# Fixing the order and metering the pace of a scan's VectorE work inside a fused SSM and feed-forward kernel

## The chip, the cores and the metric

One core of one Trainium2 chip. The metric is the device time of one execution in microseconds (us). "The span" is the time from the first to the last instruction in the profile; it lies 1 to 2 us under the measured time. Lower is better.

The engines are called PE (TensorE, the matmuls), DVE (VectorE), ACT (ScalarE), POOL (GpSimd) and SP (SyncE, which here only issues transfers).

## The reference, cut to what matters

```python
xn = layernorm(x)                                    # 2048 x 1024
# A: state-space model (SSM), 1024 complex states
Bu = einsum("bld,pd->blp", xn, B_bar)                # complex
for t in range(2048):                                # the scan
    h = Lam_bar * h + Bu[:, t]
y  = 2.0 * einsum("blp,dp->bld", hseq, C).real + xn * Dskip
# B: feed-forward network (FFN), 1024 -> 3584 -> 1024
f  = (silu(xn @ w_gate) * (xn @ w_up)) @ w_down
out = x + y + f
```

The kernel turns the complex scan into two real ones: each block of 128 states and 512 time steps (a *unit*, 32 in all) is rotated by a table of cosines and sines, scanned with a real decay, and rotated back. The tables are built by doubling, on DVE.

## The kernel before

Four parts matter: the start (load x, layernorm, transpose x through PE), the B matmuls as one block, the scan on DVE, and the FFN. The source writes the whole scan ahead of the FFN; a scheduler that models the engines decides in what order each engine really gets its instructions. The two products that the FFN needs from DVE carry a high priority.

```python
with tc.tile_pool(name="ph0_x", bufs=2, side="right") as ph0x, ...:
    for j4 in range(0, NTT, JTB):                     # four chunks of x, 1 MB each
        xt = ph0x.tile([P128, JTB, D], BF16, name="xt", tag="xt")
        nc.sync.dma_start(xt[:], x_view[:, j4 : j4 + JTB, :])
        xts.append(xt)
    nc.sync.dma_start_transpose(BT[:, 0, :, :], A_B_re)   # all of B at once
    nc.sync.dma_start_transpose(BT[:, 1, :, :], A_B_im)
    # ... per chunk: sums (ACT), squares (DVE), normalise (DVE), 32 transposes (PE),
    #     eight evictions of the transposed x into xnT (ACT)

for blk in range(NPB):                                # 8 blocks of states
    for tb in range(NTB):                             # 4 blocks of time
        ups = bups.tile([P128, 2, TBLK], FP32, name="ups", tag="ups")
        # ... 16 matmuls of 128x128x512; eviction by ACT; store to u_dram

for g in range(NPG):                                  # two blocks of states at a time
    # ... build the tables (DVE, six operations per doubling)
    for bb in range(NBG):
        for tb in range(NTB):
            # ... one unit on DVE: 6 products, 2 scans, 4 small carries, 6 products;
            #     load of u and store of h by POOL

for tq in range(NTQ):                                 # FFN, four quarters of the rows
    for fpair in range(NFP):                          # 14 pairs, 28 gate/up blocks
        # ... loads of wg and wu (pool f_w, bufs=2), 16 matmuls, 3 evictions (ACT)
        with tc.high_priority(offset=BOOST):
            nc.vector.tensor_tensor(out=gsb[:], in0=gsb[:], in1=sig[:], op=ALU.mult)
            nc.vector.tensor_tensor(out=prodT[...], in0=gsb[:], in1=usbf[:], op=ALU.mult)
    for q in range(NQ):                               # down projection, 448 matmuls
        # ...
# output stage: 4 reads of h (2 MB each), 512 matmuls with C, sum, store
```

## Time and profile before

| | before |
|---|---|
| time, median of the first 4 runs | 919.9 us (918.99 to 921.04) |
| span | 918.5 us |
| PE busy | 827.7 us (90%) |
| DVE busy | 477.8 us (52%) |
| PE work at full speed (worked out in the prediction) | 810.4 us |
| lost: start / middle / tail | 46.8 / 57.1 / 4.2 us |

PE is the engine that should never pause. DVE's 52% is an average of two stages: nearly full until about 360 us, nearly empty after. The prediction shows the slices and the pauses; it has 57.4 and 3.9 for the last two losses, but the last matmul of the lines that it shows ends at 914.35 us, 4.2 before the end of the span. Two more views help. First, the shares of the chain that ended last, in the kernel before:

```profile
PE 65%; DVE 26%; issue 3%; DMA 3%; SPq 1%; ACT 0%; POOL 0%; POOLq 0%; DVEq 0%
```

A quarter of the path to the end runs through DVE, though PE is the busier engine. Second, what PE waited for in the kernel before (total us, times, longest us):

```profile
PE gps L378 <- ACT gsb L395: 24.1, 11, 15.3
PE gps L378 <- DMA wg<-in_B_w_gate_dram: 15.7, 2, 15.2
PE dps L412 <- DVE prodT L400: 7.6, 3, 3.4
```

The first line names ACT, but ACT itself was waiting for a tile that DVE's products had not yet released.

### The profile page before, as it was taken

The page shows a single profiled execution, that of the slowest core. Times are in us where ns is not written, and L with a number is a line of the kernel's source. Part 1 is how long each engine was busy: PE and PEld are TensorE (multiplying, and loading weights), DVE is VectorE, ACT ScalarE, POOL GpSimd, SP SyncE. Part 2 cuts the span into 40 slices and gives each one's busy share as a digit, 9 for nine tenths or more (in the row PEclk, how much of TensorE's full clock was granted, in tenths as well). Part 3 has the DMA queues.
Part 4 walks back from the last instruction along what each step waited for, and adds up shares of the span by engine and source line. Part 5 has one row for each costly group of instructions (what it writes and reads, how often), then busy time and mean ns, then how long its engine had stood idle before and what let it go on. Part 6 is the DMA issues. An engine that isn't in the chain of part 4 may idle for free.

```text
span 918.5 us, 12444 instructions
## 1 busy us (share of the span) xinstructions
PE 827.7 (90%) x4736; PEld 461.8 (50%) x4736; DVE 477.8 (52%) x1291; ACT 286.2 (31%) x508; POOL 38.7 (4%) x74
## 2 busy tenths in 40 slices
PE   0669999759887897599999999999999999999998
PEld 0334444324333784244488544468744458844443
DVE  5799999999999997022200122210022220076563
ACT  5662332234433113144421354431244541100000
POOL 1002101100110100000000000000000000000000
PEclk9979999969999899699999999999999999999999
DMA  9997433865664483955546754546665523356631
GB/s 232 232 193 237 141 112 138 247 198 162 201 185 143 139 238 129 314 143 145 159 137 168 197 158 138 161 124 182 178 173 147 149 80 101 103 172 209 207 109 42
DMA packets 239788, 152.08 MB, mean 166 GB/s; under 512 B 38960, under 2 KB 219184, under 8 KB 239728
## 3 DMA queue, kind: packets, MB, share of 16 engines
q1 hardware_dynamic: 220608, 121.65, 48.3%
q0 software_dynamic: 5296, 17.05, 5.7%
q10 hardware_dynamic: 13824, 12.59, 4.1%
q8 instruction: 37, 0.61, 0.3%
q14 instruction: 23, 0.19, 0.1%
HBM read 117.71 MB, written 25.17 MB: 156 GB/s over the span
## 4 chain that ended last, share of the span: by engine, by line
PE 65%; DVE 26%; issue 3%; DMA 3%; SPq 1%; ACT 0%; POOL 0%; POOLq 0%; DVEq 0%
PE dps L412 21%; PE gps L378 15%; PE upsf L386 15%; PE yacc L455 12%; DVE ww L322 4%; DVE ln_scr L194 1%; DMA wg<-in_B_w_gate_dram 1%; DMA xt<-in_A_x_dram 1%; DVE prodT L400 1%; DVE gsb L399 1%; SPq L369 1%; DVE vv L319 1%; DMA lre_b<-in_A_Lambda_re_dram 1%; DVE ectab L278 1%; DVE hst L345 1%
## 5 line engine op out<-in xcount | busy, mean ns | idle before, releaser
L378 PE MATMUL gps<-xnT,wg 128*128 128x512 bf16 x896 | 215.0, 383 | 40.0 <-ACT gsb L395 24.1
L386 PE MATMUL upsf<-xnT,wu 128*128 128x512 bf16 x896 | 213.0, 381 | 0.0
L412 PE MATMUL dps<-wdq,prodT 128*128 128x256 bf16 x1792 | 198.4, 274 | 7.6 <-DVE prodT L400 7.6
L412 PEld LDWEIGHTS <-prodT 128*128 128x128 bf16 x1792 | 175.9, 98 | 30.2 <-DVE prodT L400 8.4
L399 DVE TENSOR_TENSOR gsb<-gsb,sig 128x512 bf16<-128x512 bf16 x112 | 47.5, 424 | 254.7 <-ACT gsb L395 254.7
L378 PEld LDWEIGHTS <-wg 128*128 128x128 bf16 x896 | 88.1, 98 | 149.8 <-issue 27.4
L386 PEld LDWEIGHTS <-wu 128*128 128x128 bf16 x896 | 88.1, 98 | 107.4 <-issue 2.9
L393 ACT ACTIVATE sig<-gps 128x512 bf16<-128x512 f32 x112 | 66.9, 597 | 168.3 <-PE gps L378 109.0
L234 PE MATMUL ups<-xnT,BT 128*128 128x512 bf16 x512 | 116.7, 383 | 0.0
L455 PE MATMUL yacc<-CT,hread 128*128 128x512 bf16 x512 | 110.7, 379 | 0.0
L397 ACT ACTIVATE usbf<-upsf 128x512 bf16<-128x512 f32 x112 | 66.8, 596 | 58.7 <-PE upsf L386 58.7
L400 DVE TENSOR_TENSOR prodT<-gsb,usbf 128x512 bf16<-128x512 bf16 x112 | 47.5, 424 | 71.0 <-ACT usbf L397 70.6
L322 DVE TENSOR_TENSOR_SCAN ww<-rdec,carry,vv 128x512 bf16<-128x512 f32 x64 | 81.9, 1283 | 0.0
L455 PEld LDWEIGHTS <-hread 128*128 128x128 bf16 x512 | 50.1, 98 | 60.2
L419 ACT ACTIVATE dstg<-dps 128x256 bf16<-128x256 f32 x64 | 24.5, 383 | 175.7 <-PE dps L412 155.4
L234 PEld LDWEIGHTS <-BT 128*128 128x128 bf16 x512 | 50.4, 99 | 56.9
L395 ACT ACTIVATE gsb<-gps 128x512 bf16<-128x512 f32 x112 | 66.5, 594 | 21.6 <-DVE prodT L400 21.6
L242 ACT ACTIVATE ust<-ups 128x1024 bf16<-128x1024 f32 x32 | 32.7, 1022 | 70.6 <-PE ups L234 65.6
L218 PE MATMUL tp<-ident,xt 128*128 128x128 bf16 x128 | 15.7, 255 | 39.0 <-DVE xt L210 37.3
L463 DVE TENSOR_TENSOR oacc<-yacc,pre 128x512 bf16<-128x512 f32 x32 | 22.1, 691 | 43.8 <-PE yacc L455 43.8
L218 PEld LDWEIGHTS <-xt 128*128 128x128 bf16 x128 | 11.3, 113 | 47.5 <-DVE xt L210 39.9
L435 DVE TENSOR_SCALAR c<-dskb,rstd 128x1024 bf16<-128x1024 bf16 x16 | 7.7, 480 | 47.8 <-PE dps L412 47.8
(104 smaller groups left out, 435.1 us busy)
## 6 DMA issues: line engine op xcount, KB each, us to landing
wg<-in_B_w_gate_dram SPq DMA_DIRECT2D x56, 512.0 KB, 3.7
wu<-in_B_w_up_dram SPq DMA_DIRECT2D x56, 512.0 KB, 4.9
wdq<-in_B_w_down_dram SPq DMA_DIRECT2D x16, 1792.0 KB, 8.7
u_dram<-ust ACTq DMA_DIRECT2D x32, 256.0 KB, 2.1
usb<-u_dram POOLq DMA_DIRECT2D x32, 256.0 KB, 3.3
h_dram<-hst POOLq DMA_DIRECT2D x32, 256.0 KB, 2.9
hread<-h_dram SPq DMA_DIRECT2D x4, 2048.0 KB, 9.9
xt<-in_A_x_dram SPq DMA_DIRECT2D x4, 1024.0 KB, 8.7
```

What stands on the lines that cost most here:

```text
L234: nc.tensor.matmul(ups[:, ri, :], lhsT=BT[:, ri, dk, blk * P128 : (blk + 1) * P128], rhs=xnT[:, dk, t0 : t0 + TBLK], start=(dk == 0), stop ...
L242: nc.scalar.activation(ust[:], ups[:], ACT.Copy)
L322: nc.vector.tensor_tensor_scan(ww[:, ri, :], rbc, vv[:, ri, :], carry[:, tb, blk, ri : ri + 1], ALU.mult, ALU.add,)
L378: nc.tensor.matmul(gps[:], lhsT=wg[:, dk, fl * P128 : (fl + 1) * P128], rhs=xnT[:, dk, tcol : tcol + TBLK], start=(dk == 0), stop=(dk == N ...
L386: nc.tensor.matmul(ups2[:], lhsT=wu[:, dk, fl * P128 : (fl + 1) * P128], rhs=xnT[:, dk, tcol : tcol + TBLK], start=(dk == 0), stop=(dk == ...
L393: nc.scalar.activation(sig[:], gps[:], ACT.Sigmoid)
L395: nc.scalar.activation(gsb[:], gps[:], ACT.Copy)
L397: nc.scalar.activation(usbf[:], ups2[:], ACT.Copy)
L399: nc.vector.tensor_tensor(out=gsb[:], in0=gsb[:], in1=sig[:], op=ALU.mult)
L400: nc.vector.tensor_tensor(out=prodT[:, ft_idx, tbq * TBLK : (tbq + 1) * TBLK], in0=gsb[:], in1=usbf[:], op=ALU.mult,)
L412: nc.tensor.matmul(dps[:], lhsT=prodT[:, ft_idx, jl * P128 : (jl + 1) * P128], rhs=wdq[:, ft_idx, :], start=(ft_idx == 0), stop=(ft_idx == ...
L455: nc.tensor.matmul(acc[:], lhsT=hread[:, blk, ri, tt * P128 : (tt + 1) * P128], rhs=CT[:, ri, blk, dh * 512 : (dh + 1) * 512], start=(i == 0),
```

## The change

The intent: let PE always have work and DVE never be late with a product. The order of instructions on DVE and on the SP queue is no longer left to the scheduler. The program writes it: after each block of PE work it emits a bounded amount of scan work, by a meter that counts PE time. The parts:

```diff
+    ph0x = tc.alloc_tile_pool(name="ph0_x", bufs=4, side="right")       # was bufs=2
+    # B is transposed per block of 128 states (bt_pool, bufs=2), not all at once
+    def emit_bu(n):
+        for _ in range(n):
+            ...                                  # one B unit: 16 matmuls, eviction, store
+        def build_table(blk): ...                # one block at a time, four operations per doubling
+        def do_unit(kcur): ...                   # 6 products, 2 scans, carries
+        def end_unit(kcur): ...                  # 6 products, store of h
+        ssm_steps = []
+        for blk in range(NPB):
+            ssm_steps.append((6.0, (lambda b=blk: build_table(b))))
+            for tb in range(NTB):
+                kk = units.index((blk, tb))
+                ssm_steps.append((5.2, (lambda k2=kk: do_unit(k2))))
+                ssm_steps.append((2.5, (lambda k2=kk: end_unit(k2))))
...
+            def advance(self, pe_us):
+                self.budget += pe_us * 0.5
+                while self.idx < len(ssm_steps) and self.budget >= ssm_steps[self.idx][0]:
+                    cost, fn = ssm_steps[self.idx]
+                    ...
+                    self.budget -= cost
+                    self.idx += 1
+                    fn()
...
+        dve_order = tc.manual_schedule(engines={mybir.EngineType.DVE, mybir.EngineType.SP})
+        dve_order.__enter__()
+        emit_bu(3)
+        ssm_driver.advance(30.0)
...
-                tc.tile_pool(name="f_w", bufs=2) as fw, \
+                tc.tile_pool(name="f_w", bufs=3) as fw, \
...
+                    if bu_state["k"] < NU:
+                        emit_bu(BU_PER_PAIR)     # three B units in each of the first pairs
...
-                            with tc.high_priority(offset=BOOST):
-                                nc.vector.tensor_tensor(out=gsb[:], ...)
+                            nc.vector.tensor_tensor(out=gsb[:], ...)
...
+                            ssm_driver.advance(GU_US + ...)      # after each gate/up block
...
+                        if tq < 2:               # C transposes, one pair per part of a down projection
+                            nc.sync.dma_start_transpose(CT[:, 0, po, :], ...)
...
+                            ssm_driver.advance(DP_US)            # after each down group
```

## The prediction

> **What bounds the kernel now.** I read the slices first, for where TensorE (PE) is not full; the stretches for how much; the PE timeline for each pause; then the chain and the groups for what the work costs when nothing is in its way.
>
> The slices of the page, 23 us each:
>
> ```profile
> PE   0669999759887897599999999999999999999998
> DVE  5799999999999997022200122210022220076563
> PEclk9979999969999899699999999999999999999999
> ```
>
> PE is at 9 from slice 18 on, and pauses only in slices 0 to 17. In just these slices VectorE (DVE) is at 9, and after slice 16 it has almost nothing to do. So the kernel is bound by PE, and what it loses, it loses while DVE works through the whole scan part of the state-space model (SSM).
>
> The stretches: bounds, length, busy us and instructions of PE, PEld, DVE, ACT, POOL, then granted clock, DMA share, GB/s:
>
> ```profile
> 0.00:69.00 69.00, 29.99 (x199) 16.59 (x200) 54.12 (x214) 43.64 (x79) 5.11 (x12) 0.90 1.03 219
> 69.00:161.00 92.00, 92.00 (x428) 41.72 (x427) 90.83 (x254) 26.60 (x26) 12.61 (x24) 1.00 0.46 156
> 161.00:391.00 230.00, 182.34 (x1025) 101.48 (x1023) 201.55 (x558) 67.43 (x123) 20.95 (x39) 0.91 0.67 196
> 391.00:804.00 413.00, 413.00 (x2579) 252.23 (x2578) 66.12 (x157) 148.28 (x280) 0.00 (x0) 1.00 0.53 147
> 804.00:914.00 110.00, 110.00 (x512) 49.81 (x509) 64.46 (x111) 0.25 (x1) 0.00 (x0) 1.00 0.46 152
> ```
>
> PE is idle 39.0 us in the first stretch and 47.7 in the third. In the fourth, 413 us, DVE has 66 us of work.
>
> What full speed is, from the chain (start, length, what) and one row of the PE timeline:
>
> ```profile
> 512.63 1.73 PE gps L378 x8
> 463.72 48.91 PE dps L412 x448
> 803.83 110.52 PE yacc L455 x512
> 63.53 100.96 PE L234 MATMUL ups<-xnT,BT 128*128 128x512 bf16 x467
> ```
>
> A gate or up group of 8 matmuls is 1.73 us (two such, one gate/up block, 3.45), a down projection 48.9, the output projection 110.5, a matmul of B times u 0.216. The work at full speed: 112 blocks x 3.454 = 386.8; 4 x 48.91 = 195.6; 110.5; 512 x 0.216 = 110.5; 128 transposes at 0.055 (four in 0.22 us in the timeline) = 7.0. Sum 810.4 us. The span is 918.5, so 108.1 are lost. Before 63.5 us PE did 45 of the B matmuls and the transposes, 16.7 us of work: 46.8 lost at the start. After the last matmul 3.9. The rest, 57.4, is lost between 164 and 391: 47.7 idle, the remainder at a lower clock and on groups cut up.
>
> The pauses themselves, in the PE timeline (in brackets the idle time before, and what ended it):
>
> ```profile
> 23.57 1.47 PE L218 MATMUL tp<-ident,xt 128*128 128x128 bf16 x6 [23.57 <-DVE xt L210]
> 52.91 1.76 PE L218 MATMUL tp<-ident,xt 128*128 128x128 bf16 x8 [13.45 <-DVE xt L210]
> 193.61 3.57 PE L378 MATMUL gps<-xnT,wg 128*128 128x512 bf16 x8 [15.31 <-ACT gsb L395]
> 249.21 1.89 PE L378 MATMUL gps<-xnT,wg 128*128 128x512 bf16 x8 [1.16 <-ACT gsb L395]
> 300.96 47.57 PE L412 MATMUL dps<-wdq,prodT 128*128 128x256 bf16 x421 [3.29 <-DVE prodT L400]
> 377.57 3.59 PE L378 MATMUL gps<-xnT,wg 128*128 128x512 bf16 x8 [15.23 <-DMA wg<-in_B_w_gate_dram]
> ```
>
> 23.57 is the first load and layernorm; 13.45 the third chunk of x, whose load could not start until one of two buffers was free (issued at 31.7 us, behind 24 us of B-transpose issue on the same queue). 15.31 and the 1.16 kind are one thing: ScalarE (ACT) waits for its tile because the two FFN products on DVE stand behind scan work. 15.23 is the queue: several 1.8 MB down weights and a 2 MB read of h were issued together, and the issue of the gate weights behind them took 11.5 us.
>
> **What the Trainium skill says.** "TensorE: Matmul & The Clock Gate", Part 1, says PE runs at half clock after an idle window of about 3.4 us until it has been busy as long. The trace agrees: after the 15.31 pause the first eight matmuls took 3.57 us, later ones 1.89, and the three long pauses are the slices at 6 and 7 of the clock row. Each long pause thus costs some 2 to 3 us more. "Perfetto Trace Analysis", Per-engine timelines, says ACT and DVE are strict FIFO; the trace agrees, as products ready for 15 us run after scan work already queued. "VectorE: DVE Perf Modes", the perf-mode tier table, caps fp32 tensor-tensor at one element per cycle and lets fp32 tensor-scalar have two; the trace has 690 ns for 512 fp32 elements of the first and 482 of the second. That bears on the new tables.
>
> **The change, part by part.** (1) All four x loads have buffers and go first; B is transposed per block of 128 rows, two small transposes each, rather than 24 us of issue at once. This takes away the 13.45 pause. What is left is the rate of ACT and DVE: ACT has 16 sums x 1.05 (start to start) + 32 evictions x 0.54 + 4 table loads x 1.28 = 39 us from 6.5 us on, five B evictions at 1.02, and I allow 3 to 4 of waits, so it ends near 54. DVE has 16 x 1.15 + 16 x 0.46 + 10 of small operations = 36 from 10 us. PE starts at 23 as before; until 54 it can do the transposes (7) and up to six B units of 3.45 (20.7): 27.7. The rest is in order behind them, and the FFN's PSUM banks overlap those of the transposes (four B banks, two for transposes, four for the FFN are more than eight). Loss at the start: 54 - 27.7 = 26, plus 2 for the cold clock and 2 for poor order: 30 in place of 46.8. Gain 17.
>
> (2) The B units are no longer a block of 92 us that only PE works in; three go in each of the first ten FFN pairs. PE's work does not change by that, gain 0 in itself. It gives DVE 92 us more FFN time to hide behind.
>
> (3) The scan is metered: after each block of PE time t it may emit t/2 of DVE work, and DVE and the SP queue run in the order written. A scan unit is 12 products at 0.335 (start to start), 2 scans at 1.20, 0.5 of carries = 7.0 us; the meter says 5.2 + 2.5. A table now has per doubling two tensor-scalars and two fused operations; about 0.55 us for each of six small levels, 0.7, 1.0 and 1.4 for the large, 2.8 for casts and the last four = near 9 us an estimate; the meter says 6. Total 32 x 7.0 + 8 x 9 = 296 us, as the meter has it (294), so it takes 590 us of PE time and ends in the fourth quarter, well ahead of the output stage. In a plain block of 3.45 us DVE has 0.75 of products and 1.73 of scan: 72%. The longest thing in front of a product is a table, 9 us. PE has two PSUM tiles and ACT two SBUF tiles of lead, so the product of block i must be done before PE wants block i+4: about 3 blocks less 2.5 us of ACT and DVE, 7.9 us after its inputs. So nearly nothing reaches PE. At the four turns to the down projection the last product is wanted 2.95 us after the block; a unit of 5 us just ahead of it costs 1 to 2, a table up to 6: 6 in all. The 15.31 and the many small pauses go.
>
> (4) SP order: the gate weights have a third buffer, 13.8 us of lead; down weights sit between weights, one per quarter of the projection, so the pile-up at 360 us does not form. The C transposes go singly into the first two down projections. I keep 3 us for the two early h reads that the scheduler may still put anywhere. Loss in the middle: 6 + 3 = 9 in place of 57.4. Gain 48.
>
> (5) The output stage and its tail are unchanged: 3.9.
>
> Sum: 810.4 + 30 + 9 + 3.9 = 853.3 us of span; the median lies 1.4 over the span (919.9 against 918.5): **855 us**, ratio 0.93.
>
> **The rivals.** First: fixed order turns into head-of-line blocking. DVE now waits for block i's ACT tiles before it may scan, and for the first scan input before the first product; ACT and PE keep the scheduler's own order, which misjudged DVE before. For: the whole 57 us of the middle came from orders that looked right to the scheduler. Against: mean DVE load of 72% and the slack of 7.9. If each of some 40 scan steps outside the B part cost 0.7, 28 more: 883. Second: the start stays as it is, because ACT is the bound there and the six B units sit in the wrong order; then 870. For: before, PE ran only 45 of the B matmuls by 63.5 though two chunks were ready. Third: the DMA pile-up moves. An h read of 2 MB (9.9 us to land) twice in the fourth quarter, or the strict SP order holding weights behind B transposes that wait for a buffer; 5 to 15 more: 860 to 870. Fourth, upwards: the start is filled perfectly and the turns cost nothing: 840.
>
> **Range and chances.** The floor is 810.4 + 23 + 3.9, near 838 with the clock. Of rivals one to three I expect half of one to happen, which fits in **842 to 884**. To miss 2% (901.5) three quarters of the gain would have to be lost. Faster 0.94, same 0.04, slower 0.02.
>
> **What would show it.** In the new profile: no PE pause over 3 us after the start; clock slices below 9 only in the first three; PE near 95% of the span; DVE's work spread at 6 to 8 tenths over slices 2 to 28, with the h stores ending near 630 us; waits of PE on ACT gsb (24.1 us now) under 5, on prodT under 8; loss before the last transpose about 30. Wrong if DVE shows waits on the scan's inputs ahead of products, if PE waits on gate weights, or if the turns to the down projection pause for over 3 us each.

## The result, and the profile after

**852.53 us** median of 8 runs (851.41 to 853.7), against 919.54 us for the kernel before (13 runs). The ratio is 0.9268, 95% interval 0.9259 to 0.9277. Ratios here are the mean time of one kernel's fast runs over that of the other's of the same rounds, so they are not quite the ratio of the medians quoted.

The slices of the kernel after, 21 us each (PE, DVE, granted PE clock):

```profile
PE   0699999999999999999999999999999999999998
DVE  5985657548679355978906588870862210366652
PEclk9999999999999999999999999999999999999999
```

PE is full from slice 2 on, and no slice of the clock row is below 9. DVE's work, once a block of 9s in front, now reaches to slice 29, at 3 to 9 tenths, with two gaps (slices 20 and 27 are at 0). The gaps show that the meter fixes the order of the work and not its time: the scan work written between the groups of a down projection waits for nothing on PE, so in the second quarter DVE ran it in one go, from 395 to 426 us, and then stood idle for 19.9 us until the next quarter's first product. The work has not become less: DVE is busy 504.4 us, 26.6 more than before. The change moved work; it removed none.

Three stretches of the kernel after, with the columns that the prediction explains:

```profile
0.00:62.05 62.05, 34.27 (x224) 18.89 (x225) 50.60 (x203) 43.77 (x80) 6.06 (x14) 0.97 0.63 164
62.05:391.00 328.95, 328.95 (x1747) 170.83 (x1746) 213.75 (x593) 126.49 (x209) 20.14 (x38) 1.00 0.68 185
391.00:640.00 249.00, 248.14 (x1594) 155.63 (x1592) 162.79 (x451) 84.65 (x163) 12.45 (x23) 1.00 0.70 186
```

From 62.05 us to the end of the third line PE is idle 0.86 us. The PE timeline of the kernel after has the start and that one pause:

```profile
24.48 0.40 PE L207 MATMUL tp<-ident,xt 128*128 128x128 bf16 x2 [24.48 <-DVE xt L199]
...
51.75 10.47 PE L237 MATMUL ups<-xnT,btsl 128*128 128x512 bf16 x47
62.05 1.89 PE L438 MATMUL gps<-xnT,wg 128*128 128x512 bf16 x8
...
543.71 46.13 PE L480 MATMUL dps<-wdq,prodT 128*128 128x256 bf16 x421 [0.86 <-DVE prodT L459]
```

By 62.05 us PE has done the transposes and six B units, 27.7 us of work at full speed: 34.3 lost. The 13.45 us pause of the third chunk is gone. All that PE waited for in the kernel after:

```profile
PE tp L207 <- DVE xt L199: 25.2, 4, 24.5
PE tp L207 <- ACT xnT L212: 2.3, 2, 1.7
PE dps L480 <- DVE prodT L459: 0.9, 1, 0.9
```

The waits on gsb and on the gate weights, 24.1 and 15.7 us before, do not occur at all. The shares of the chain, kernel after:

```profile
PE 94%; DVE 3%; DMA 1%; ACT 1%; issue 0%; POOL 0%; DVEq 0%; POOLq 0%; ACTq 0%
```

DVE's 26% has become 3%. The account closes to 0.4 us: 810.4 of work, 34.3 lost at the start, 0.9 in the middle and 3.6 in the tail give 849.2, and the span is 849.6 us. Of the 68.9 us gained in span, 12.5 come from the start, some 56 from the middle and half a us from the tail.

The last store of h, in the POOL timeline of the kernel after:

```profile
633.56 0.54 POOL L368 DMA_DIRECT2D h_dram<-hst  x1 [14.96 <-DVE hst L367]
```

It is issued some 100 us before the output stage needs h.

### The profile page after: what moved, and what is told of

Same layout as the page of the kernel before. It is cut to its first block, busy times and chain, and to the rows that moved or that the text cites.

```text
span 849.6 us, 12534 instructions
## 1 busy us (share of the span) xinstructions
PE 817.3 (96%) x4736; PEld 460.2 (54%) x4736; DVE 504.4 (59%) x1387; ACT 284.5 (33%) x508; POOL 38.7 (5%) x74
## 4 chain that ended last, share of the span: by engine, by line
PE 94%; DVE 3%; DMA 1%; ACT 1%; issue 0%; POOL 0%; DVEq 0%; POOLq 0%; ACTq 0%
PE dps L480 23%; PE upsf L446 22%; PE gps L438 22%; PE yacc L527 13%; PE ups L237 13%; DVE ln_scr L183 1%; PE tp L207 1%; DMA lre_b<-in_A_Lambda_re_dram 1%; ACT ln_scr L181 0%; DVE ww L330 0%; ACT xnT L212 0%; DVE xt L199 0%; DVE prodT L459 0%; DVE oacc L535 0%; DVE gsb L458 0%
## 5 line engine op out<-in xcount | busy, mean ns | idle before, releaser
L438 PE MATMUL gps<-xnT,wg 128*128 128x512 bf16 x896 | 211.7, 379 | 0.0
L237 PE MATMUL ups<-xnT,btsl 128*128 128x512 bf16 x512 | 119.2, 383 | 0.1
L237 PEld LDWEIGHTS <-btsl 128*128 128x128 bf16 x512 | 50.3, 99 | 56.9 <-issue 1.1
L330 DVE TENSOR_TENSOR_SCAN ww<-rdec,carry,vv 128x512 bf16<-128x512 f32 x64 | 78.5, 1268 | 0.0
L535 DVE TENSOR_TENSOR oacc<-yacc,pre 128x512 bf16<-128x512 f32 x32 | 22.1, 691 | 43.8 <-PE yacc L527 43.8
L207 PE MATMUL tp<-ident,xt 128*128 128x128 bf16 x128 | 15.4, 249 | 27.7 <-DVE xt L199 25.2
L264 POOL DMA_DIRECT2D usb<-u_dram x32 | 17.2, 538 | 325.0 <-DVE rt L326 245.1
```

The source lines that it names most:

```text
L237: nc.tensor.matmul(ups[:, ri, :], lhsT=btsl[:, ri, dk, :], rhs=xnT[:, dk, t0 : t0 + TBLK], start=(dk == 0), stop=(dk == ND - 1),)
L330: nc.vector.tensor_tensor_scan(ww[:, ri, :], rbc, vv[:, ri, :], carry[:, tb, blk, ri : ri + 1], ALU.mult, ALU.add,)
L438: nc.tensor.matmul(gps[:], lhsT=wg[:, dk, fl * P128 : (fl + 1) * P128], rhs=xnT[:, dk, tcol : tcol + TBLK], start=(dk == 0), stop=(dk == N ...
```

## The experiments

My theory: the middle gain needs *both* the fixed order on DVE and a pace that DVE can hold; the start gain is the two further x buffers; spreading the B units is worth nothing in itself. Rivals: the interleaving of B carries the gain, or the order of SP does, or the meter alone (the scheduler would then manage), or the order alone.

### Fixed order taken away: e1_free_order

```diff
-        dve_order = tc.manual_schedule(engines={mybir.EngineType.DVE, mybir.EngineType.SP})
-        dve_order.__enter__()
...
-        dve_order.__exit__(None, None, None)
```

> The kernel after, with the region that fixes the order on DVE and on the SP queue taken away; the meter, the interleaved B units and the start stay. Theory A (the meter's place in the program is what counts, the scheduler then mostly keeps it): 850 to 862 us, PE waits on ACT gsb under 5 us. Rival B (the fixed order is what counts; left to itself the scheduler again lets DVE run scan work ahead of FFN products, as in the kernel before): 870 to 910 us, with PE pauses on ACT gsb and prodT as before.

905.66 us, ratio 0.9841 (0.9826 to 0.9856): of the 67 us gained, 15 are left, about what the start alone brings (e8, below). The DVE row of its slices, then its PE waits:

```profile
DVE  5989999999999999222200222210022220075563
```

```profile
PE gps L436 <- ACT gsb L453: 22.4, 4, 10.6
PE dps L478 <- DVE prodT L457: 8.8, 3, 3.6
```

The meter's place in the program is not kept: DVE is at 9 from slice 3 to 15, and the waits on gsb and prodT are back at their old size. The change also dropped the high priority of the products, so this run has neither order nor priority. Without both, the gain of the middle is gone. The kernel before had the priority without the meter and lost 57 us in the middle; meter and priority together, without the fixed order, were not tried, so that rival stays untested.

### Fixed order on DVE alone: e2_dve_order_only

```diff
-tc.manual_schedule(engines={mybir.EngineType.DVE, mybir.EngineType.SP})
+tc.manual_schedule(engines={mybir.EngineType.DVE})
```

> The kernel after with the order fixed on DVE only, the SP queue left to the scheduler. If the SP order matters (the pile-up of down weights and h reads in front of gate weights comes back, 15.2 us in the kernel before): 862 to 870 us with one PE pause on gate weights near 10 to 15 us. If only the DVE order matters: within 3 us of 852.5.

852.81 us, ratio 0.9265 (0.9251 to 0.9279), the same as the whole change. PE's waits on weights were 0.6 and 0.2 us. The SP half of the fixed order did nothing here.

### The pace: e3_meter_1, e5_meter_035, e11_meter_065

```diff
-                self.budget += pe_us * 0.5
+                self.budget += pe_us * 1.0        # e3; 0.35 in e5, 0.65 in e11
```

> The kernel after with the meter at 1.0 us of scan per us of PE time in place of 0.5, order fixed. Theory (the meter keeps DVE under PE's pace): in a plain block DVE then has 0.75 + 3.45 = 4.2 us against PE's 3.45, so PE is paced by DVE until the scan is done; the scan is done after some 290 us of PE time, most of it in the B part, where a pair has 17.3 of scan + 1.5 of products against 17.3 of PE: 15 us of lag over ten pairs, about half of it swallowed by the buffers, then some ten plain blocks at 0.75 each. 860 to 875 us. Rival (the fixed order alone, at any pace, gives the gain): within 3 us of 852.5.

913.71 us, ratio 0.9933 (0.9916 to 0.9949). That is 39 us over the upper end of what I expected. Slices, then two waits of PE:

```profile
DVE  5999999999999999972200122210022220076563
```

```profile
PE gps L438 <- ACT gsb L455: 24.3, 8, 7.6
PE ups L237 <- ACT ust L245: 12.4, 4, 5.1
```

With fixed order but twice the pace, DVE is full until about 400 us and the products are late again. What was wrong in the expectation, the DVE timeline of this run shows, one whole unit between two pairs of products:

```profile
202.92 0.42 DVE L321 TENSOR_TENSOR vv<-gtab,usb 128x512 bf16<-128x512 bf16 x1
203.25 0.42 DVE L322 TENSOR_TENSOR rt<-gtab,usb 128x512 bf16<-128x512 bf16 x1
203.70 0.42 DVE L323 TENSOR_TENSOR vv<-vv,rt 128x512 bf16<-128x512 bf16 x1
...
211.55 0.42 DVE L321 TENSOR_TENSOR vv<-gtab,usb 128x512 bf16<-128x512 bf16 x1
```

From one unit to the next is 8.63 us; less 0.86 for the two products between them, a unit takes 7.77, where I had 7.0. In written order an operation often follows the one that it depends on, and then starts 0.45 us after it (203.25 to 203.70) instead of 0.33 (202.92 to 203.25). In the kernel before, whose 0.335 I had used for all products, the scheduler put other operations between such neighbours: there one whole unit, carries included, takes 6.89 us (180.59 to 187.48 in its DVE timeline). So the written order itself costs DVE 0.88 us a unit. The next unit, one of the 8 without carries, took 6.88, and a table, between its neighbours in the same timeline, 10.55. So the whole scan takes 24 x 7.77 + 8 x 6.88 + 8 x 10.55 = 326 us, where the meter counts 294: each metered us costs 1.11. Per gate/up block, in which the meter counts 3.41 us and PE takes 3.45, DVE needs 0.86 + 1.11 x 3.41 x pace. That is 2.75 at pace 0.5 (80%), 3.32 at 0.65 (96%) and 4.65 at 1.0 (135%). Pace 1.0 cannot be held. In the expectation's own sum a pair with B units is then 3.6 us late and not 1.5, and a plain block 1.2 and not 0.75: by its own counts 48 us of lag where I had 22 (an estimate). This run is 61 us slower than the change; the rest is not worked out.

> The kernel after with the meter at 0.65. From the run with the meter at 1.0: 1.11 us of DVE per metered us, 0.86 for the two products; a plain block then has 0.86 + 3.45 x 0.65 x 1.11 = 3.35 us of DVE against 3.45 of PE. Theory (only a DVE load over 100% reaches PE): 851 to 860 us. Rival (what hurt at 1.0 is single steps in front of a product, not the load): over 865 us.

857.15 us, ratio 0.9322 (0.9308 to 0.9336), in the range expected. At 96% nothing reaches PE within the blocks, but one turn to a down projection does. The PE timeline, then the stretches from 404 to 408 us:

```profile
404.01 0.61 PE L480 MATMUL dps<-wdq,prodT 128*128 128x256 bf16 x2 [3.14 <-DVE prodT L459]
```

```profile
404.00:406.00 2.00, 1.73 (x8) 1.10 (x9) 1.93 (x6) 0.66 (x2) 0.00 (x0) 0.50 0.11 33
406.00:408.00 2.00, 2.00 (x11) 1.42 (x10) 1.97 (x6) 0.00 (x0) 0.55 (x1) 0.50 0.32 113
```

The clock stayed at 0.50 until about 410 us, 6 us of PE work, so the pause of 3.14 us cost about 6 in all. The DVE timeline shows what stood in front: a table from 385.23 to 395.77 us made the next products late, and the first part of a unit, from 397.50 to 403.01, lay just ahead of the last ones, which ended the pause. So the theory that only a load over 100% reaches PE is not quite right: at 96%, single long steps ahead of a turn did.

> The kernel after with the meter at 0.35. The FFN and B parts hold 702 us of metered PE time, so 246 of the scan's 294 metered us are placed in them and 49 are left for the end; with those of the last down projection 65 metered us run after the last FFN product near 688 us, and DVE took 1.11 us per metered us in the run with the meter at 1.0, so DVE ends the scan near 760, when the output projection wanted h at 737. Theory (too slow a meter is paid at the end, unhidden): 865 to 885 us, one PE pause of 15 to 30 us ahead of the output projection. Rival (any pace under PE's will do): within 3 us of 852.5.

898.94 us, ratio 0.9777 (0.9763 to 0.9792): worse than expected by 14 us, by the mechanism expected. One line of its PE timeline says it:

```profile
780.68 0.59 PE L527 MATMUL yacc<-CT,hread 128*128 128x512 bf16 x1 [46.23 <-DMA hread<-h_dram]
```

By the meter's own constants PE's work before the output stage counts 30 + 112 x 3.41 + 92 for B + 64 x 2.99 = 695 us. At 0.35 that pays for 243 of the 294; the rest is emitted at the end in one piece and PE waits. The pace must be above 294 / 695 = 0.42 (an estimate from the constants), and by the sum above below about (3.45 - 0.86) / (1.11 x 3.41) = 0.68. The 0.5 of the change lies between: 899 at 0.35, 852.5 at 0.5, 857 at 0.65, 914 at 1.0.

### The B units in one block again: e6_b_first

```diff
-        emit_bu(3)
-        ssm_driver.advance(30.0)
+        emit_bu(NU)
+        ssm_driver.advance(30.0 + (NU - 3) * BU_MM_US)
```

> The kernel after with all 32 B units emitted ahead of the FFN, as in the kernel before; the meter is advanced by the same PE time for them, so DVE gets the same share. The prediction said that the interleaving is worth nothing in itself: 850 to 860 us. Rival (the interleaving is what hides the scan, or PE needs the FFN blocks between them): over 870 us.

850.97 us, ratio 0.9246 (0.9232 to 0.926). All B units before the FFN, with the meter advanced by as much, is no slower than spreading them. "Perfetto Trace Analysis", Optimization Strategy, says that a kernel with several regimes may gain by interleaving them. Here interleaving B with the FFN gave nothing (0.9268 with it, 0.9246 without): B was PE work with DVE free to scan beside it, wherever it stood. What e1 and e3 show to matter is how much scan work stands ahead of each product.

### The third weights buffer: e7_two_weight_bufs

```diff
-                tc.tile_pool(name="f_w", bufs=3) as fw, \
+                tc.tile_pool(name="f_w", bufs=2) as fw, \
```

> The kernel after with two buffers for gate and up weights in place of three. Theory (the pauses of the middle came from DVE's order, the third buffer is slack only): 851 to 858 us. Rival (the third buffer is what took away the 15.2 us pause on gate weights): 862 us or more, with a PE pause on gate weights at a turn from down projection to gate and up.

858.59 us, ratio 0.9337 (0.9323 to 0.9351): 6 us slower than the change, a little over what I expected. In its PE timeline:

```profile
649.74 3.53 PE L438 MATMUL gps<-xnT,wg 128*128 128x512 bf16 x8 [3.94 <-DMA wg<-in_B_w_gate_dram]
```

Eight matmuls take 3.53 us here, against 1.90 later in the same timeline: the pause and the cold clock (half speed) after it are most of the 6 us. It falls just after the scan's end, where the early h reads share the SP queue with the weights. The issue of the second h read took 3.83 us, from 643.96 on, and this wg was issued right behind it, at 647.89. With three buffers the weights are issued earlier and the same reads cost nothing, though the issue of the second took 7.11 us there.

### The x buffers alone, in the kernel before: e8_before_x4

```diff
-            with tc.tile_pool(name="ph0_x", bufs=2, side="right") as ph0x, \
+            with tc.tile_pool(name="ph0_x", bufs=4, side="right") as ph0x, \
```

> The kernel before with four buffers for x in place of two, nothing else. Theory (the 13.45 us pause was the third chunk waiting for a buffer): the pause goes, 904 to 912 us. Rival (the start is bound by ACT and DVE and by 24 us of B-transpose issue, so the time comes back at once): 915 us or more.

907.55 us, ratio 0.9869 (0.9853 to 0.9886). The 13.45 us pause is gone; the middle is as it was, as its PE timeline shows:

```profile
182.07 1.44 PE L378 MATMUL gps<-xnT,wg 128*128 128x512 bf16 x3 [14.99 <-ACT gsb L395]
```

These two buffers give 12 us, nearly all that the start gained in the whole change (12.5). By the last transpose 35.4 us are lost here, 34.1 in the change and 46.8 in the kernel before, so transposing B in pieces and the rest of the new start can have added about 1 us.

### What bounds the start: e13_ln_order, e14_ln_order_bt3, e15_split_evict, e16_ln_split_evict

34.3 us are still lost at the start, where I had 30. All four are built on e6. In e13 the layernorm is written ahead of the SSM's parameters, with DVE in that order; e14 adds a third buffer for B.

```diff
+    ln_order = tc.manual_schedule(engines={mybir.EngineType.DVE})
+    ln_order.__enter__()
+    ...                                   # layernorm and transposes moved here
     nc.vector.tensor_copy(lre[:], lre_b[:])   # SSM parameters follow
...
-    btp = tc.alloc_tile_pool(name="bt_pool", bufs=2, side="right")
+    btp = tc.alloc_tile_pool(name="bt_pool", bufs=3, side="right")    # e14 only
```

> The kernel with the B units first (851.0 us), in which the layernorm also comes ahead of the SSM parameters in the program and DVE's order is fixed through both, so that the first DVE instruction no longer waits for the parameters' load. Theory (half of what is left at the start, 24.5 us to the first transpose, is DVE's order: parameter operations and the second chunk's sums run ahead of the first chunk's normalisation): first transposes near 13 us, 840 to 848 us. Rival (the start is bound by the rate of ACT and DVE over all four chunks, which stays): first transposes earlier, but the time within 3 us of 851.

> The same with three buffers for the transposed blocks of B in place of two, so that PE has nine to twelve B units to choose from while the later chunks of x are normalised. If PE runs out of B units at the start: 3 to 6 us below the run with two. If ACT's evictions hold it: within 2 us of it.

851.51 us (ratio 0.9267, 0.9251 to 0.9282) and 851.73 us (0.9266, 0.9253 to 0.928): no gain, though in e13 the first transpose starts at 16.11 us instead of 24.59. Two stretches of e13:

```profile
24.00:36.00 12.00, 9.06 (x66) 4.46 (x65) 10.34 (x24) 12.00 (x25) 0.00 (x0) 1.00 0.01 3
36.00:48.00 12.00, 6.14 (x44) 3.57 (x44) 6.91 (x22) 11.89 (x19) 0.55 (x1) 0.72 0.11 27
```

ACT is full, 12.00 and 11.89 of 12 us, and PE then paused 4.72 us for the last chunk's normalisation, for which DVE had itself waited 2.75 us on ACT. So ACT's rate looked like the bound, and e15 relieves it: every second eviction of the transposed x goes to DVE, in e6 itself. e16 does the same in e14, with the layernorm of the next chunk (sums, squares and normalisation) written ahead of the evictions.

```diff
-                nc.scalar.activation(xnT[:, dk, ...], tp[:], ACT.Copy)
+                if dk % 2 == 0:
+                    nc.scalar.activation(xnT[:, dk, ...], tp[:], ACT.Copy)
+                else:
+                    nc.vector.tensor_copy(xnT[:, dk, ...], tp[:])
```

> The kernel with all B units ahead of the FFN, with every second eviction of the transposed x (odd dk, 16 of 32) done by VectorE instead of ScalarE. Theory: ScalarE's rate bounds the start (it was busy 12.0 of 12 us between 24 and 36 us when the layernorm came earlier). 16 evictions of 0.54 us off it free about 8.6 us there, and VectorE has room; the first transpose still starts near 24.6 us, so not all of it shows: 844 to 849 us against 851. Rival: the start is bound by when the first chunk of x is normalised (24 us) and by the order behind it, not by ScalarE: within 1.5 us of 851.

> The kernel with the layernorm first on VectorE in fixed order and three buffers for the transposed B, with every second eviction on VectorE as well, and the statistics of the next chunk written ahead of the evictions of the present one, so that they don't queue behind them. There the first transpose already starts at 16 us and ScalarE alone held the rest. Theory: with the two bounds gone together, last eviction near 46 us instead of 53, and 843 to 848 us against 851.7. Rival: the two loads behind x on the queue (B transposes) or VectorE's fixed order hold it now: within 1.5 us of 851.7.

851.68 us (ratio 0.9262, 0.9249 to 0.9274): no gain, against the theory. 858.62 us (0.9335, 0.9322 to 0.9347): 7 us worse, against both. The same two stretches of e15:

```profile
24.00:36.00 12.00, 8.78 (x58) 4.57 (x60) 12.00 (x66) 10.11 (x21) 0.00 (x0) 1.00 0.00 1
36.00:48.00 12.00, 9.63 (x81) 5.25 (x79) 11.88 (x60) 5.89 (x10) 0.84 (x2) 1.00 0.20 68
```

Now ACT has room (16.0 of 24 us) and DVE is full (23.9 of 24). But in e6, from which it starts, DVE had been busy 22.6 of these 24 us and ACT 22.1, and a part of DVE's work there is parameters and tables for the scan, which the start does not need. In e16 neither is full (DVE 17.3, ACT 13.1 of those 24 us), and PE waits three times (15.0 us in all) for an eviction on DVE. I had written the next chunk's squares and normalisation ahead of it: in the first case DVE was at them until 25.66 us, while both PSUM tiles of the transposes stood full. The first two of these waits in the PE timeline of e16:

```profile
26.12 1.01 PE L164 MATMUL tp<-ident,xt 128*128 128x128 bf16 x8 [5.32 <-DVE xnT L173]
...
39.30 1.01 PE L164 MATMUL tp<-ident,xt 128*128 128x128 bf16 x8 [5.49 <-DVE xnT L173]
```

So "ACT's rate bounds the start" falls. What the four show: with DVE's order eased ACT is full, with ACT eased DVE is full (which does not yet prove that it is the bound), and with both eased my written order made its own waits. Whether a better order would bring the start under 34 us stays open.

No version clearly beat the change. e6 was the fastest at 850.97 us; its interval just overlaps that of the change, and the difference is 0.2%.

## Why the prediction was right

- **The bound and the full-speed sum (810.4 us): right.** The account of the kernel after closes to 0.4 us with it. The tail was misread by 0.3: 4.2 us before and 3.6 after, where I had 3.9 for both.
- **Start, gain 17: mechanism right, size off.** 12.5 measured, and e8 shows that the x buffers are nearly all of it. The last eviction by ACT ended at 53.4 us, where I had 54. But PE began at 24.48 us and not at 23, and by the end of the transposes, at 51.75, it had done 17.6 us of work; 47 of the 96 B matmuls ran after that, until 62.05 us. From its first transpose on PE had lost 9.7 us, where I had left 7.3: 3.3 of waiting (23 to 54 us, less 27.7 of work), 2 for the cold clock and 2 for poor order. The loss was 34.3 instead of 30.
- **Middle, gain 48: mechanism right, size off the other way.** I left 6 us for the turns to the down projections and 3 for early h reads. The turns cost 0.86 in all, the h reads nothing. Both costs do exist close by: a turn cost 3.14 and a cold clock at pace 0.65, and e7 paused for 3.94 on a gate weight. The change has just enough reserve. The two errors of size, +4.3 and -8.1, partly cancel: 849.6 of span for 853.3. That the number came within 3 us is in part luck.
- **Interleaving B, gain 0 in itself: shown by e6.** The "92 us more FFN time to hide behind" was worth nothing either.
- **SP order and third buffer: half right.** The pile-up did not form, and the third buffer is worth 6 us (e7). The fixed order of SP, to which I gave part of it, is worth nothing (e2).
- **DVE's sums: too low.** A unit takes 7.77 and not 7.0, a table 10.55 and not 9, the scan 326 and not 296 us. At pace 0.5 this hid in the reserve, and the last h store came at 633.56 us, for "near 630". The step that failed is taking 0.335 us per product from an order that the scheduler had interleaved and using it for a written one. It is the larger part of what spoiled my expectation of e3.
- **First rival, head-of-line blocking:** it did not occur at 0.5, and does once the pace is too high (e3). It also did in e16, at the start.
- **What would show it:** no PE pause over 3 us after the start, PE at 96%, no wait on gsb, 0.9 on prodT, all as written; the clock did better (no slice under 9), and DVE's tenths were 3 to 9, with two slices at 0, rather than 6 to 8. "Loss before the last transpose about 30" named the right place: it was 34.1 there, and 34.3 at the first FFN matmul.

## What to carry to other kernels

Filler work for a half-empty engine needs two things, and here neither was enough alone: a fixed place between the urgent operations (without it, and without the priority, 906 us; with it 852.5), and a pace below what the engine can hold (at pace 1.0 914 us in the same fixed order). Bound the pace from both sides before choosing it: from above by the engine's time per block less its urgent work, with durations taken from *neighbouring dependent* operations and some room for the longest single step, from below by when the result is wanted. Moving work between two nearly full engines gained nothing at the start here (e15), so look at both engines' rows first.

## What the Trainium skill lacked or had wrong

- "VectorE: DVE Perf Modes", The DRAIN you can't avoid: it says that a semaphore between two operations costs nothing extra, measured there on copies, and that the next one, where it is not held, starts before the pipe is empty. The second agrees: an independent bf16 operation of 512 elements starts 0.33 us after the last, which is recorded as running for 0.42. But one that depends on its neighbour starts 0.45 us after it, a third more; whether a semaphore or something else holds it, the views used here do not show. The four dependent products make up some 0.5 of the 0.8 us between the 7.77 of a scan unit and my 7.0.
- "TensorE: Matmul & The Clock Gate", Part 1: it gives about 3.4 us for the idle window and as much for the busy one, and says that the window runs free of the kernel. The long pauses agree, but in e11 a pause of 3.14 us sufficed, and PE then worked for about 6 us at 0.50 before the clock came back. So 3.4 is no sharp limit for a single pause or a single warm-up.
- No page that I read has the price of writing an engine's order by hand: 0.86 us of PE pause in the whole kernel where the pace fits, 15 us in three pauses where an eviction stood behind a chunk's layernorm (e16), and on DVE 7.77 us for a scan unit in place of 6.89 in the scheduler's order.
